# The last tokens of the second pair in the free half of the first pair's last slot: linear attention and a gated feed-forward layer on one core

## The chip, the cores and the metric

The kernel runs on one core of a Trainium2 chip. The metric is the time of one execution on the device in microseconds (us). Engines: PE is TensorE (matmuls and transposes; PEld is its weight load, which overlaps), DVE is VectorE, ACT is ScalarE, POOL is GpSimd, SP is SyncE, from which most transfers are issued. PSUM is the memory that PE writes its results to; ACT and DVE read it.

## The reference

There are 8 batches of 8 heads, with 576 tokens of 64 numbers each, all float32. The attention has no softmax:

```python
kv = np.einsum('bhsd,bhse->bhde', k, v)
out = np.einsum('bhsd,bhde->bhse', q, kv)
rms = np.sqrt(np.mean(out * out, axis=-1, keepdims=True) + 1e-06)
x = out / rms * g_norm          # (8, 8, 576, 64), then to (4608, 512)
```

The feed-forward layer follows, with d_model 512 and d_ff 1536. Its weights come as float64 and are converted on the chip.

```python
gate = 1.0 / (1.0 + np.exp(-(x @ w_gate)))
return (gate * (x @ w_val)) @ w_out
```

## The kernel before

Heads are taken two at a time: a *pair* n is two heads of one batch, so a batch has four pairs (NHP = 4) and there are 32 pairs in all. The tokens of the feed-forward layer come in nine *chunks* of 512 (G), the transposed activations of a chunk lying in the tile xT (chunk(c) makes it). A batch of 576 tokens crosses a chunk's edge.

**Steps of a pair** (attention, L229 to L310). They are kv_mm and kv_out (the 64x64 matrix kv of each head), q_mm (Q, six transposes of q to a PSUM tile, L251), q_out (ACT copies them to the tile qT, L256), u_mm (U, out = q kv, L271), u_square (ACT, L276), u_sum (DVE, L280), u_root (ACT, L284), u_norm (DVE, reciprocal and product, L288 and L290), x_mm (X, transposes with the identity matrix, L298) and x_out (X_OUT, ACT copies to xT with the factor g_norm, L307).

**Slots of tokens.** The 576 tokens of a pair are laid out in NU = 5 slots of 128 partitions, and each slot has 64 columns for each head. U works in groups of 64 tokens: groups 0, 2, 4, 6, 8 go to the lower 64 partitions of the five slots, groups 1, 3, 5, 7, 9 to the upper ones. There are nine groups of tokens but ten places: group 9 takes `t0 = min(PH * i, S - PH)`, that is the tokens of group 8 once more, so the upper half of the last slot holds a copy that nobody reads. A group is two matmuls, one for each head, and each matmul is 64 rows by 64 columns of the array; so the matmuls of two groups in a row take the array's four quadrants in turn. The trace has two records for each such matmul.

**Early and late pairs.** The first eight pairs (NE = 8, two batches) are done in an order written out by hand (`order`, L458), with PSUM tiles of their own. The other 24 pairs, those of batches 2 to 7, run underneath the feed-forward layer. For these, `feed(b)` (L319) puts the steps of the batch's four pairs into the queue `fill`. It takes two pairs at a time, one and two_ (called a couple here), in this order: Q and Q_OUT of one, the same of two_; for the first couple of the batch the kv of all four pairs, of the whole batch, after up to three empty steps; then U of both in one step, Square of both, sum of both, root and norm of one, root and norm of two_, X and X_OUT of one, X and X_OUT of two_. A batch has two couples, so there are twelve.

**The loop around them.** For each chunk c from 1 to 8, `feed(c + 1)` fills the queue, then the first layer (first_layer_fast, products at L578) and the second layer (second_layer_fast, products at L664) are recorded. Both layers use a scheme with seven products of half size (p1 to p7). After every two products of the first layer (eight matmul records on PE) `slot()` takes one step from `fill`. At c = 1 the queue also holds sums of the second layer's weights, spread between the steps. All engines work their instructions off in the order in which they are recorded, so the position in `fill` is the position in the queues of PE, ACT and DVE.

**PSUM tiles of the late pairs.** `at_ps` gives them out in turn from two buffers, at and at1, each with two banks:

```python
    def at_ps(kind):
        if next(turns) % 2 == 0:
            return at0_ps()
        return psum.tile([P, 2, 512], FP32, tag="at1", name="at1")
```

Each of Q, U and X takes one tile for each pair, so that one always has at and two_ has at1 (the trace calls both "at"). A new tile in a buffer waits until the readers of the previous one there are done.

**X and X_OUT.** X transposes the five slots into the PSUM tile: slots 0 to 2 into columns 0 to 383 of bank 0, slots 3 and 4 into columns 0 to 255 of bank 1. X_OUT copies columns 0 to 383 of bank 0 and 0 to 191 of bank 1, with one more cut where a chunk of 512 tokens ends: two pieces in batch 2, three in the batches after.

Of the kernel before, what the change touches and what calls it, by code (L numbers as in the profile page):

```python
# [10 lines left out]
FP32 = mybir.dt.float32  # L11
# [3 lines left out]
AF = mybir.ActivationFunctionType  # L15
ALU = mybir.AluOpType
AX = mybir.AxisListType
# [3 lines left out]
def kernel(  # L21
# [11 lines left out]
    nc = tc.nc  # L33

    B, H, S, HD = q.shape
    T, DM = out.shape
    DF = moe_w_gate.shape[1]
    P = 128
# [5 lines left out]
    PH = P // 2  # L44
    NU = -(-S // P)
    UX = P * 3

    NK4 = S // P
    S4 = P * NK4
# [3 lines left out]
    G = 512  # L53
# [5 lines left out]
    sb = ctx.enter_context(tc.tile_pool(name="sb", bufs=2))  # L59
# [9 lines left out]
    NE = 2 * NHP  # L69
# [66 lines left out]
    one = const.tile([P, 1], FP32, name="one")  # L136
# [74 lines left out]
    g_col = const.tile([P, 1], FP32, name="g_col")  # L211

    kvs = [const.tile([P, 2, HD], FP32, name=f"kv{i}") for i in range(2)]
# [10 lines left out]
    def chunk(c):  # L224
        if c not in xT:
            xT[c] = sb.tile([P, NMT, G], FP32, tag="xT", name="xT", bufs=3)
        return xT[c]

    def attention(n, at_ps):  # L229

        b, m = divmod(n, NHP)
        d = {}
        kv = kvs[n // 2 % 2][:, n % 2]

        def kv_mm():
            d["kv"] = ps = at_ps("kv")
            for j in range(NJ):
                js = slice(HD * j, HD * j + HD)
                for e in range(2):
                    nc.tensor.matmul(ps[HD * e:HD * e + HD, 0, 0:HD], pairs[n]["k"][:, e, js], pairs[n]["v"][:, e, js],  # L240
                                     start=(j == 0), stop=(j == NJ - 1))

        def kv_out():
            nc.vector.tensor_copy(out=kv, in_=d["kv"][:, 0, 0:HD])
            load_kv(n + 4)

        def q_mm():
            d["q"] = ps = at_ps("q")
            for j in range(NJ):
                c0 = NP * (j % JH)  # L250
                nc.tensor.transpose(ps[:, j // JH, c0:c0 + NP], pairs[n]["q"][:, j].rearrange("p e d -> p (e d)"),  # L251
                                    ident[0:NP, 0:NP])

        def q_out():
            d["qT"] = sb.tile([P, 2, JH * NP], FP32, tag="qT", name="qT")
            nc.scalar.copy(out=d["qT"], in_=d["q"][:, :, 0:JH * NP])  # L256
            for i in (n + 4,) if n + 4 < NE else (n + 2,) if n + 2 >= NE else ():
                load_q(i)

        def u_mm():  # L260


            ps = at_ps("u")
            d["u"] = ps[:, :, 0:NU * HD]
            qT = d["qT"].rearrange("p i n -> p (i n)")
            for i in range(2 * NU):
                t0 = min(PH * i, S - PH)
                r = PH * (i % 2)
                for e in range(2):
                    es = slice(HD * e, HD * e + HD)  # L270
                    nc.tensor.matmul(d["u"][r:r + PH, e, HD * (i // 2):HD * (i // 2) + HD], qT[es, t0:t0 + PH], kv[es],  # L271
                                     start=True, stop=True)

        def u_square():
            d["sq"] = sb.tile([P, 2, NU * HD], FP32, tag="sq", name="sq")
            nc.scalar.activation(out=d["sq"], in_=d["u"], func=AF.Square)  # L276

        def u_sum():
            d["ms"] = sb.tile([P, 2, NU], FP32, tag="ms", name="ms")
            nc.vector.tensor_reduce(out=d["ms"].rearrange("p e i -> p (e i)"),  # L280
                                    in_=d["sq"].rearrange("p e (i d) -> p (e i) d", d=HD), axis=AX.X, op=ALU.add)

        def u_root():
            nc.scalar.activation(out=d["ms"], in_=d["ms"], func=AF.Sqrt, bias=eps, scale=1.0 / HD)  # L284

        def u_norm():

            nc.vector.reciprocal(d["ms"], d["ms"])  # L288
            d["xn"] = d["sq"].rearrange("p e c -> p (e c)")
            nc.vector.tensor_tensor(out=d["xn"].rearrange("p (i e d) -> p e i d", e=2, d=HD),  # L290
                                    in0=d["u"].rearrange("p e (i d) -> p e i d", d=HD),
                                    in1=d["ms"].unsqueeze(3).to_broadcast([P, 2, NU, HD]), op=ALU.mult)

        def x_mm():
            d["x"] = ps = at_ps("x")
            for i in range(NU):
                bank, c0 = divmod(P * i, UX)
                nc.tensor.transpose(ps[:, bank, c0:c0 + P], d["xn"][:, P * i:P * i + P], ident)  # L298

        def x_out():  # L300

            s0 = 0
            while s0 < S:
                c, o = divmod(S * b + s0, G)
                i, r = divmod(s0, UX)
                n_ = min(G - o, (UX if i == 0 else S - UX) - r)
                nc.scalar.activation(out=chunk(c)[:, m, o:o + n_], in_=d["x"][:, i, r:r + n_], func=AF.Copy, scale=g_col)  # L307
                s0 += n_

        return [kv_mm, kv_out, q_mm, q_out, u_mm, u_square, u_sum, u_root, u_norm, x_mm, x_out]  # L310


# [6 lines left out]
    def feed(b):  # L319

        early = b == 2
        d = {}

        def kv_mm():
            mains, rest = kv_late[b]
            tiles = [at_ps("kv") for _ in range(2)]
            d["kv"] = tiles
            for n in range(NHP):
                for j in range(NK4):
                    for e in range(2):  # L330
                        c = slice(NK4 * HD * e + HD * j, NK4 * HD * e + HD * j + HD)
                        nc.tensor.matmul(tiles[n // 2][HD * e:HD * e + HD, n % 2, 0:HD], mains[n, "k"][:, c],  # L332
                                         mains[n, "v"][:, c], start=(j == 0), stop=False)
            for i in range(NHP // 2):
                for r in range(2):
                    for e in range(2):
                        n, rs, c = NHP // 2 * r + i, slice(PH * r, PH * r + PH), HD * (2 * i + e)
                        nc.tensor.matmul(tiles[n // 2][HD * e:HD * e + HD, n % 2, 0:HD], rest[rs, c:c + HD],
                                         rest[rs, GH + c:GH + c + HD], start=False, stop=True)

        def kv_out():
            for kv, ps in zip(kvs, d["kv"]):
                nc.vector.tensor_copy(out=kv, in_=ps[:, :, 0:HD])

        def idle():
            pass

        for n in range(NHP * b, NHP * b + NHP, 2):
            one, two_ = (attention(n + i, at_ps) for i in range(2))

            def u_of_both(one=one, two_=two_):
                one[U]()
                two_[U]()

            fill.extend([one[Q], one[Q_OUT], two_[Q], two_[Q_OUT]])
            if n == NHP * b:
                fill.extend([idle] * (0 if early else 3) + [kv_mm, kv_out])
            fill.extend([u_of_both, one[U_SQUARE], two_[U_SQUARE], one[U_SUM], two_[U_SUM], one[U_ROOT], one[U_NORM],
                         two_[U_ROOT], two_[U_NORM], one[X], one[X_OUT], two_[X], two_[X_OUT]])
# [32 lines left out]
    def at0_ps():  # L392
        return psum_at.tile([P, 2, 512], FP32, tag="at", name="at")
# [3 lines left out]
# [5 lines that stand above are left out]
    def early(n):  # L402

        shared = []

        def ps(kind):
            if kind == "q":
                return shared[0]
            t = psum0.tile([P, 2, 512], FP32, tag="kq" if kind == "kv" else f"ux{n % 2}", name="two")
            if kind == "kv":  # L410
                shared.append(t)
                return t[:, :, JH * P:]
            return t
        return ps

    def mm_ps():
        return psum.tile([P, 512], FP32, tag="mm", name="mm", bufs=4)
# [30 lines left out]


    KV, KV_OUT, Q, Q_OUT, U, U_SQUARE, U_SUM, U_ROOT, U_NORM, X, X_OUT = range(11)  # L450
    a = [attention(n, early(n)) for n in range(NE)]

    steps = {"KV": KV, "KVO": KV_OUT, "Q": Q, "QO": Q_OUT, "U": U, "SQ": U_SQUARE, "SUM": U_SUM, "ROOT": U_ROOT,
             "NORM": U_NORM, "X": X, "XO": X_OUT}
# [16 lines left out]
    for token in order.split():  # L471
        name = token.rstrip("0123456789.")
        n = [int(i) for i in token[len(name):].split(".")]
        f = n[0]
        if name == "b":
            if f not in blks:
                if f == 3:
                    psum_ctx.__exit__(None, None, None)
                    psum = ctx.enter_context(tc.tile_pool(name="psum", bufs=1, space=bass.MemoryType.PSUM))
                    ps = (mm_ps(), mm_ps())  # L480
                else:
                    t = at0_ps() if f else two0
                    ps = (t[:, 0], t[:, 1])
# [35 lines left out]
    ps = [two1[t % 2][:, t // 2] for t in range(G // P)]  # L519
# [259 lines left out]
```

## Time and profile before

| what | value |
|---|---|
| median of 4 runs | 1097.14 us (1096.53 to 1099.04) |
| the profiled execution | 1099.04 us, span of its instructions 1097.2 us |
| granted PE clock | 0.998 of full speed |
| busy, share of the span | PE 99%, DVE 51%, ACT 29%, POOL 25% |
| products of the first layer, L578 | 53% of the chain that ended last |
| products of the second layer, L664 | 26% of it |
| L271, L298 and L251 on "at" (late pairs) | 1% each or less |
| late pairs: first Q, last X_OUT | from 164.6 us to 834.4 us |

The span runs from the first to the last instruction of the program. A matmul's record includes the pipeline's tail, so that records of PE overlap; what one costs is seen from its start to the next start. "Idle before" and "waits" name the engine whose signal came last.

### The profile page before, as it was taken

To read this page: it belongs to the slowest core of one execution; us is meant where nothing else is said; L and a number is where in the kernel's file an instruction comes from. 1 tells how busy PE (TensorE), PEld (TensorE's weight loads), DVE (VectorE), ACT (ScalarE), POOL (GpSimd) and SP (SyncE) were. 2 spreads that over 40 slices of the span, in tenths; PEclk is the share of its full clock that TensorE was granted. 3 is DMA by queue.
4 is the path that set the end of the run, shared out by engine and by line. 5 is a ranking of instruction groups with operands and counts; after the bars stand their busy time and mean duration, and the time that the engine had idled before them with its cause. 6 is when DMAs were issued, how large, how long until landed. Compare 5 with 4: busy or idle time off the path is not lost.

```text
span 1097.2 us, 17063 instructions
## 1 busy us (share of the span) xinstructions
PE 1089.7 (99%) x6722; PEld 903.1 (82%) x6722; DVE 564.1 (51%) x1117; ACT 316.1 (29%) x611; POOL 279.2 (25%) x390
## 2 busy tenths in 40 slices
PE   8999999999999999999999999999999999999998
PEld 7544448888888888888888888888888888888888
DVE  3787855763365416561466336641656155615641
ACT  4654322431244113430254014511443011101110
POOL 0000023440244203440344024420334044404410
PEclk9999999999999999999999999999999999999999
DMA  9954711000400040001400040104000100010001
GB/s 230 246 191 153 240 29 33 1 23 20 127 1 22 11 120 19 22 1 36 112 22 1 20 127 1 23 10 121 18 1 1 29 10 1 1 36 4 1 1 39
DMA packets 81519, 57.73 MB, mean 53 GB/s; under 512 B 47392, under 2 KB 75424, under 8 KB 81440
## 3 DMA queue, kind: packets, MB, share of 16 engines
q1 hardware_dynamic: 81184, 56.61, 19.3%
q8 instruction: 54, 0.88, 0.3%
q14 instruction: 25, 0.20, 0.1%
q10 hardware_dynamic: 256, 0.03, 0.0%
HBM read 47.19 MB, written 9.44 MB: 52 GB/s over the span
## 4 chain that ended last, share of the span: by engine, by line
PE 97%; DMA 1%; DVE 1%; SPq 1%; issue 0%; ACT 0%; DVEq 0%
PE mm L578 53%; PE mm L664 26%; PE mm L427 6%; PE at L522 4%; PE at L271 1%; PE at L427 1%; DMA q<-in_q_dram 1%; PE at L298 1%; PE at L332 1%; PE at L251 1%; PE at L506 1%; PE two L271 0%; PE two L251 0%; PE two L298 0%; PE two L240 0%; SPq L78 0%
## 5 line engine op out<-in xcount | busy, mean ns | idle before, releaser
L565 POOL TENSOR_TENSOR tw<-gv 128x256 f32<-128x256 f32 x192 | 138.8, 734 | 767.8 <-PE mm L578 614.0
L578 PE MATMUL mm<-xT,tw 128*128 128x256 f32 x768 | 182.2, 380 | 0.2 <-DVE gv L592 0.2
L578 PE MATMUL mm<-sx,tw 128*128 128x256 f32 x768 | 182.3, 380 | 0.0
L578 PE MATMUL mm<-xT,gv 128*128 128x256 f32 x768 | 181.8, 380 | 0.0
L578 PEld LDWEIGHTS mm<-xT,gv 128*128 128x128 f32 x768 | 144.8, 190 | 19.7 <-issue 0.5
L578 PEld LDWEIGHTS mm<-xT,tw 128*128 128x128 f32 x768 | 144.1, 190 | 19.6 <-issue 0.6
L578 PEld LDWEIGHTS mm<-sx,tw 128*128 128x128 f32 x768 | 144.2, 190 | 19.0
L565 POOL TENSOR_TENSOR tw<-gv,tw 128x256 f32<-128x256 f32 x192 | 146.1, 784 | 0.0
L610 ACT ACTIVATE sg<-sg 128x256 f32<-128x256 f32 x96 | 40.0, 417 | 190.2 <-DVE sg L609 190.2
L600 DVE TENSOR_TENSOR gv<-mm,sg 128x256 f32<-128x256 f32 x96 | 40.8, 424 | 103.1 <-PE mm L578 103.1
L578 PE MATMUL mm<-sx,gv 128*128 128x256 f32 x384 | 91.3, 381 | 0.0
L664 PE MATMUL mm<-w,gv 128*128 128x256 f32 x384 | 88.5, 379 | 0.4 <-DVE gv L617 0.4
L664 PE MATMUL mm<-w,s 128*128 128x256 f32 (+1 forms) x408 | 88.3, 367 | 0.0
L664 PE MATMUL mm<-t2w,gv 128*128 128x256 f32 x384 | 88.1, 379 | 0.0
L586 ACT COPY sg<-mm 128x256 f32<-128x256 f32 x96 | 35.8, 373 | 165.9 <-PE mm L578 162.0
L617 DVE TENSOR_TENSOR gv<-gv,sg 128x512 f32<-128x512 f32 x96 | 82.7, 901 | 0.0
L664 PEld LDWEIGHTS mm<-w,s 128*128 128x128 f32 x408 | 74.1, 190 | 9.4
L664 PEld LDWEIGHTS mm<-w,gv 128*128 128x128 f32 x384 | 72.8, 190 | 10.6 <-DVE gv L617 0.8
L664 PEld LDWEIGHTS mm<-t2w,gv 128*128 128x128 f32 x384 | 72.9, 190 | 9.9
L578 PEld LDWEIGHTS mm<-sx,gv 128*128 128x128 f32 x384 | 72.5, 190 | 10.0
L596 ACT ACTIVATE sg<-mm 128x256 f32<-128x256 f32 x96 | 36.2, 384 | 106.1 <-PE mm L578 106.1
L614 DVE TENSOR_TENSOR gv<-mm,gv 128x256 f32<-128x256 f32 x96 | 40.7, 424 | 48.1 <-PE mm L578 48.1
(97 smaller groups left out, 1094.0 us busy)
## 6 DMA issues: line engine op xcount, KB each, us to landing
q<-in_q_dram SPq DMA_DIRECT2D x64, 144.0 KB, 3.3
st<-in_moe_w_gate_dram SPq DMA_DIRECT2D x12, 512.0 KB, 4.3
st<-in_moe_w_val_dram SPq DMA_DIRECT2D x12, 512.0 KB, 5.3
st<-in_moe_w_out_dram SPq DMA_DIRECT2D x12, 512.0 KB, 4.6
kv<-in_k_dram SPq DMA_DIRECT2D x24, 256.0 KB, 5.1
kv<-in_v_dram SPq DMA_DIRECT2D x24, 256.0 KB, 5.4
out_dram<-sg SPq DMA_DIRECT2D x23, 192.0 KB, 2.3
out_dram<-sg SPq DMA_DIRECT2D x24, 128.0 KB, 2.4
```

The source lines that it names most:

```text
L251: nc.tensor.transpose(ps[:, j // JH, c0:c0 + NP], pairs[n]["q"][:, j].rearrange("p e d -> p (e d)"), ident[0:NP, 0:NP])
L427: nc.tensor.matmul(self.ps[i], w[("wg", "wv")[i], self.f][:, m, :], xT[self.c][:, m, :], start=(m == 0), stop=(m == NMT - 1), skip_group_c ...
L522: nc.tensor.matmul(ps[t], gv[0, f][:, P * t:P * t + P], w["wo", f], start=(f == 0), stop=(f == NFT - 1), skip_group_check=True)
L565: nc.gpsimd.tensor_tensor(out=tw[f, i], in0=b[in0], in1=b[in1] if isinstance(in1, tuple) else tw[f, in1], op=ALU.subtract)
L578: nc.tensor.matmul(ps, wt[:, m, :], xs[:, m, :], start=(new and m == 0), stop=(m == NK - 1), skip_group_check=True)
L586: nc.scalar.copy(out=d["sg"][:, h2], in_=pa)
L596: nc.scalar.activation(out=d["sg"][:, h1], in_=d["pa"], func=AF.Sigmoid)
L600: tt(out=d["h"][:, h2], in0=d["pb"], in1=d["sg"][:, h2], op=ALU.add)
L610: nc.scalar.activation(out=d["sg"][:, h2], in_=d["sg"][:, h2], func=AF.Sigmoid)
L614: tt(out=d["h"][:, h1], in0=d["pc"], in1=d["h"][:, h1], op=ALU.add)
L617: tt(out=d["h"], in0=d["h"], in1=d["sg"], op=ALU.mult)
L664: nc.tensor.matmul(ps, hs(f), ws[:, f, :], start=(new and f == 0), stop=(f == NF2 - 1), skip_group_check=True)
```

## The change

For the late pairs, the second pair of each couple gives up its fifth slot. Its last 64 tokens go to the upper half of the first pair's fifth slot, where the copy was.

- `attention` gets the dictionary d from outside, and `mate` (for two_: the dictionary of one) and `alone`. With a mate, a pair has nu = 4 slots, else 5.
- U of one makes eight groups instead of ten. U of two_ first makes two groups into one's tile: one's last tokens (lower half) and its own last tokens (upper half). Then it makes its own eight.
- Square, sum, root, norm and X of two_ work on four slots, those of one on five as before; one's fifth slot now carries the last tokens of both.
- X_OUT of two_ copies tokens 0 to 383 and 384 to 511 from its own tile, and tokens 512 to 575 from columns 192 to 255 of bank 1 of one's tile. It has one piece more than before.
- The early pairs are called with neither mate nor alone=False and keep their ten groups and five slots. Line numbers behind the edit move (Q is L252, X is L304 and X_OUT is L316 in the changed kernel).

```diff
-    def attention(n, at_ps):
+    def attention(n, at_ps, d, mate=None, alone=True):
...
-        d = {}
-        kv = kvs[n // 2 % 2][:, n % 2]
+        d["kvs"] = kv = kvs[n // 2 % 2][:, n % 2]
+        nu = NU - 1 if mate else NU
...
-            for i in range(2 * NU):
-                t0 = min(PH * i, S - PH)
+            d["u"] = at_ps("u")[:, :, 0:nu * HD]
+            def group(i, of, t0, into):
                 r = PH * (i % 2)
+                qT = of["qT"].rearrange("p i n -> p (i n)")
                 for e in range(2):
                     es = slice(HD * e, HD * e + HD)
-                    nc.tensor.matmul(d["u"][r:r + PH, e, HD * (i // 2):HD * (i // 2) + HD], qT[es, t0:t0 + PH], kv[es],
-                                     start=True, stop=True)
+                    nc.tensor.matmul(into["u"][r:r + PH, e, HD * (i // 2):HD * (i // 2) + HD], qT[es, t0:t0 + PH],
+                                     of["kvs"][es], start=True, stop=True)
+            if mate:
+                for i, of in ((2 * NK4, mate), (2 * NK4 + 1, d)):
+                    group(i, of, S4, mate)
+            for i in range(2 * NU if alone else 2 * NK4):
+                group(i, d, min(PH * i, S4), d)
...
-            for i in range(NU):
+            for i in range(nu):
                 bank, c0 = divmod(P * i, UX)
                 nc.tensor.transpose(ps[:, bank, c0:c0 + P], d["xn"][:, P * i:P * i + P], ident)
...
+            sources = [(UX, d["x"][:, 0]), (S4 if mate else S, d["x"][:, 1])]
+            if mate:
+                sources.append((S, mate["x"][:, 1, P * NU - UX - PH:]))
+            first_, s0 = 0, 0
+            for end, src in sources:
+                while s0 < end:
+                    c, o = divmod(S * b + s0, G)
+                    n_ = min(G - o, end - s0)
+                    nc.scalar.activation(out=chunk(c)[:, m, o:o + n_], in_=src[:, s0 - first_:s0 - first_ + n_],
+                                         func=AF.Copy, scale=g_col)
+                    s0 += n_
+                first_ = end
...
-            one, two_ = (attention(n + i, at_ps) for i in range(2))
+            d0, d1 = {}, {}
+            one, two_ = attention(n, at_ps, d0, alone=False), attention(n + 1, at_ps, d1, d0, False)
```

More of the change, by code (lines that the diff above doesn't have):

```diff
@@ L260, in u_mm @@
         def u_mm():
-            ps = at_ps("u")
-            d["u"] = ps[:, :, 0:NU * HD]
-            qT = d["qT"].rearrange("p i n -> p (i n)")
-            for i in range(2 * NU):
-                t0 = min(PH * i, S - PH)
+            d["u"] = at_ps("u")[:, :, 0:nu * HD]
+            def group(i, of, t0, into):
                 r = PH * (i % 2)
+                qT = of["qT"].rearrange("p i n -> p (i n)")
                 for e in range(2):
                     es = slice(HD * e, HD * e + HD)
-                    nc.tensor.matmul(d["u"][r:r + PH, e, HD * (i // 2):HD * (i // 2) + HD], qT[es, t0:t0 + PH], kv[es],
-                                     start=True, stop=True)
+                    nc.tensor.matmul(into["u"][r:r + PH, e, HD * (i // 2):HD * (i // 2) + HD], qT[es, t0:t0 + PH],
[5 more added lines that the diff above has]
+                group(i, d, min(PH * i, S4), d)
         def u_square():
-            d["sq"] = sb.tile([P, 2, NU * HD], FP32, tag="sq", name="sq")
-            nc.scalar.activation(out=d["sq"], in_=d["u"], func=AF.Square)
+            d["sq"] = sb.tile([P, 2 * NU * HD], FP32, tag="sq", name="sq")[:, 0:2 * nu * HD]
+            nc.scalar.activation(out=d["sq"].rearrange("p (e c) -> p e c", e=2), in_=d["u"], func=AF.Square)
         def u_sum():
-            d["ms"] = sb.tile([P, 2, NU], FP32, tag="ms", name="ms")
-            nc.vector.tensor_reduce(out=d["ms"].rearrange("p e i -> p (e i)"),
-                                    in_=d["sq"].rearrange("p e (i d) -> p (e i) d", d=HD), axis=AX.X, op=ALU.add)
+            d["ms"] = sb.tile([P, 2, NU], FP32, tag="ms", name="ms")[:, :, 0:nu]
+            nc.vector.tensor_reduce(out=d["ms"], in_=d["sq"].rearrange("p (e i d) -> p e i d", e=2, d=HD), axis=AX.X,
+                                    op=ALU.add)
         def u_root():
@@ L288, in u_norm @@
             nc.vector.reciprocal(d["ms"], d["ms"])
-            d["xn"] = d["sq"].rearrange("p e c -> p (e c)")
+            d["xn"] = d["sq"]
             nc.vector.tensor_tensor(out=d["xn"].rearrange("p (i e d) -> p e i d", e=2, d=HD),
                                     in0=d["u"].rearrange("p e (i d) -> p e i d", d=HD),
-                                    in1=d["ms"].unsqueeze(3).to_broadcast([P, 2, NU, HD]), op=ALU.mult)
+                                    in1=d["ms"].unsqueeze(3).to_broadcast([P, 2, nu, HD]), op=ALU.mult)
         def x_mm():
             d["x"] = ps = at_ps("x")
-            for i in range(NU):
+            for i in range(nu):
                 bank, c0 = divmod(P * i, UX)
@@ L300, in x_out @@
         def x_out():
[L302 to L308, printed above, removed]
+            sources = [(UX, d["x"][:, 0]), (S4 if mate else S, d["x"][:, 1])]
[10 more added lines that the diff above has]
+                first_ = end
         return [kv_mm, kv_out, q_mm, q_out, u_mm, u_square, u_sum, u_root, u_norm, x_mm, x_out]
@@ L450 @@
     KV, KV_OUT, Q, Q_OUT, U, U_SQUARE, U_SUM, U_ROOT, U_NORM, X, X_OUT = range(11)
-    a = [attention(n, early(n)) for n in range(NE)]
+    a = [attention(n, early(n), {}) for n in range(NE)]
     steps = {"KV": KV, "KVO": KV_OUT, "Q": Q, "QO": Q_OUT, "U": U, "SQ": U_SQUARE, "SUM": U_SUM, "ROOT": U_ROOT,
```

## The prediction

> **What bounds the kernel now.** I read the page's engine shares and chain first, then what PE waits for after 160 us, where the changed code runs, and then the timeline around each changed step.
>
> ```profile
> PE 1089.7 (99%) x6722; PEld 903.1 (82%) x6722; DVE 564.1 (51%) x1117; ACT 316.1 (29%) x611; POOL 279.2 (25%) x390
> PE 97%; DMA 1%; DVE 1%; SPq 1%; issue 0%; ACT 0%; DVEq 0%
> ```
>
> The first line is busy time by engine, the second the chain that ended last. TensorE is the bound: whatever leaves its queue shortens the span one for one, and whatever makes it wait lengthens it so. The waits of PE between 160 us and the end are two in all:
>
> ```profile
> PE mm L664 <- DVE gv L617: 0.4, 1, 0.4
> PE mm L578 <- DVE gv L592: 0.2, 1, 0.2
> ```
>
> So ACT, DVE and the DMA queues are hidden there, and the question is only what PE issues and what it will newly wait for. The change touches the 24 late pairs, twelve couples (one, two_); the first eight pairs issue the same instructions as before, and no DMA is added, moved or made smaller.
>
> **Removed from PE.** Here are the U block of a couple (all 80 matmul records of both pairs), an X block, and each time the row after it.
>
> ```profile
> 182.14 1.40 PE L271 MATMUL at<-kv,qT 64*64 64x64 f32 x80
> 183.46 0.70 PE L578 MATMUL mm<-xT,gv 128*128 128x256 f32 x2
> ...
> 213.94 0.71 PE L298 MATMUL at<-ident,sq 128*128 128x128 f32 x5
> 214.49 0.81 PE L578 MATMUL mm<-xT,tw 128*128 128x256 f32 x3
> ```
>
> Columns are start, duration, instruction; a matmul's duration includes the pipeline's tail, so cost is read from start to next start. U: 40 matmuls, two records each, take 183.46 − 182.14 = 1.32 us. The single starts inside show groups of four records 7 ns apart (the four quadrants of the array), and 58.5 ns from one group of four to the next. The change leaves 36 matmuls: one's first eight groups (16), then the two last groups, one's into the lower and two_'s into the upper half (4), then two_'s eight (16). The quadrants still rotate, so whole groups of four leave: 8 records, 2 × 58.5 = 117 ns. (An even share of the block, 8/80 of 1.32, would be 132; I take the starts.) X: five transposes take 0.55 us, 109 ns each; two_ keeps four. Per couple 117 + 109 = 226 ns, twelve couples: **−2.71 us**.
>
> Here a rule speaks against the change. The Trainium skill (TensorE: Matmul & The Clock Gate, Part 3: Packing small matmuls) gives a further tile in one packed group about 4 ns. By it eight records would save an estimated 32 ns instead of 117, and the sum would end 1.0 us higher. The trace shows 7 ns inside a group and 58.5 ns from group to group, which speaks for the larger figure as long as whole groups leave.
>
> **Smaller on DVE and ACT.** Square, reduce and normalize of two_ shrink from 640 to 512 columns. PE's work covers this, except at one place before PE's 0.2 us wait at 197.8:
>
> ```profile
> 196.49 0.81 DVE L280 TENSOR_REDUCE ms<-sq 128x10 f32<-128x640 f32 x1
> 197.22 0.74 DVE L592 TENSOR_TENSOR gv<-mm,sg 128x256 f32<-128x256 f32 x2
> 197.78 1.53 PE L578 MATMUL mm<-xT,tw 128*128 128x256 f32 x6 [0.23 <-DVE gv L592]
> ```
>
> This reduce is two_'s, and PE waits for the DVE queue just behind it. Gains between 0 and a fifth of 0.81 (0.16); 128 columns at about 1 ns, as L617's 0.68 us for 512 columns against 0.42 for 256 has it, make **−0.13 us**, once. The other wait (L617 at 247.4) stands behind one's normalize, which keeps its size.
>
> **Added: a fourth eviction, and a wait on it.** X_OUT of two_ must now read its last 64 columns from one's PSUM tile: its last piece of 192 becomes 128 and 64. More important, one's tile ("at") is thereby held until two_'s last piece, and the next step but one, Q of the next couple, writes a new tile into that buffer. Before, that Q needed only one's X_OUT, over by 3.7 us. Each batch of late pairs has one such boundary, between its two couples: six in all. (After the second couple the next Q is 30 us away or more.) Five look like the first three rows here, and the one of chunk 1 like the last three:
>
> ```profile
> 446.23 1.05 ACT L307 ACTIVATE xT<-at,g_col 128x256 f32<-128x256 f32 x3
> 447.22 0.69 PEld L251 LDWEIGHTS at<-ident,q 96*128 96x128 f32 x6
> 447.43 0.66 PE L251 MATMUL at<-ident,q 96*128 96x96 f32 x6
> ...
> 217.20 0.88 ACT L307 ACTIVATE xT<-at,g_col 128x384 f32<-128x384 f32 x2
> 217.73 0.69 PEld L251 LDWEIGHTS at<-ident,q 96*128 96x128 f32 x6
> 217.94 0.66 PE L251 MATMUL at<-ident,q 96*128 96x96 f32 x6
> ```
>
> The pieces end at 447.28, just 0.15 us before Q's first transpose; at chunk 1 they end at 218.07, 0.13 after it. The added piece by form:
>
> ```profile
> L307 ACT ACTIVATE xT<-at,g_col 128x192 f32<-128x192 f32 x32 | 12.6, 422 | 0.3 <-PE at L298 0.2
> L307 ACT ACTIVATE xT<-at,g_col 128x128 f32<-128x128 f32 x8 | 2.9, 364 | 0.3 <-PE at L298 0.2
> L307 ACT ACTIVATE xT<-at,g_col 128x64 f32<-128x64 f32 x8 | 2.5, 310 | 0.3 <-PE at L298 0.2
> ```
>
> 364 + 310 − 422 = 252 ns, less the overlap of two pieces in a row (starts lie about 0.10 us before the end of the one ahead): 0.15 us. So the pieces end at 447.43 and 218.22. What ACT to PE then takes is seen early in the run, where PE does wait for ACT:
>
> ```profile
> 7.75 0.64 ACT L256 COPY qT<-two 128x576 f32<-128x576 f32 x1 [4.29 <-DVE kv L244]
> 8.43 0.60 PEld L271 LDWEIGHTS two<-kv,qT 64*64 64x64 f32 x33 [0.48 <-ACT qT L256]
> ```
>
> 8.38 to 8.43: 0.05 us to the weight load; from there to the first transpose after a wait is 0.03 (load 6.73, transpose 6.76), and the second then follows 109 ns later instead of 87, so 0.02 more. Five boundaries: 447.43 + 0.08 + 0.02 − 447.43 = 0.10 each; chunk 1: 218.22 + 0.08 + 0.02 − 217.94 = 0.38. Sum **+0.90 us**. The start of the pieces hangs on PE itself (the copy of L586 or sigmoid of L610 ahead of them waits for first-layer products), so it shifts with PE and the distances hold. Behind the waiting Q stand, in order, all first-layer matmuls, and for those DVE, ACT and POOL. Bounds: −0 (the wait never last) and the rivals below. One's Square still becomes ready at the 20th matmul; ACT's extra 0.15 us per couple is otherwise free at 29% busy, and would cost 12 × 0.15 = 1.8 us without that cover.
>
> Sum: −2.71 − 0.13 + 0.90 = **−1.94 us**. The profiled execution took 1099.04 us, span 1097.2, so 1097.1 by its own time; it was the slowest of four runs, 1.9 above their median 1097.14. Against the median: **1095.2 us**, 0.18% less. A measurement of this kernel can tell about 0.2% (2.2 us) from no change, so this lies close below that edge.
>
> **Rivals.**
> Covered: the fourth piece does not bite, because ACT's signal goes out before the recorded end. Then −2.84: 1094.3. For it: five boundaries miss by only 0.1 us; against: chunk 1 already ends 0.13 late.
> Dearer seams: after U blocks the trace has a second product starting 320 ns after the first instead of 216; such a restart, 0.104 at each of six boundaries, gives −1.32: 1095.8. Or the mixed group, which takes weights from two qT tiles, loses its overlap and runs at the two-at-a-time rate that the KV block shows (59 ns for two records): +0.117 × 12 = 1.4, so −0.54: 1096.6.
> Slower: Q's wait, at the same six places, costs a slot. If the pieces started one slot later (1.73 us for the eight records of a slot), six boundaries would cost about 10.4 us: 1104.7. It decides from (2.84 + 2.2)/6 = 0.84 us per boundary on, against 0.15 on average in my sum. For: the eviction sits one slot ahead of Q, with no other step between; against: nothing new stands before the pieces on ACT.
> That PE's work does not shrink is ruled out by the order of the changed build: 60 matmuls fewer, 36 per U block, nine transposes per couple.
>
> **How the numbers follow.** Forecast 0.45, covered 0.30, dearer seams 0.18, slower 0.07. Runs scatter by 0.6 us below the median. Faster by over 0.2%: nearly all of covered (0.28), 0.20 of the forecast with that scatter, 0.02 of the seams, 0.50. Slower: 0.07. The rest is 0.43. Low end: −2.71 and all of the 0.39 us that the matmul after the wait at 197.8 came late, 1094.0, less 0.6: 1093.4. High end: 1096.6 plus 0.6: 1097.2.
>
> **What would show it.** Right: U blocks of 72 records in about 1.21 us; X of two_ in 0.44; a new row of PE or PEld at "at", Q's line, waiting for ACT xT, six times, some 0.9 us with chunk 1 the longest; from the first Q of one middle batch to that of the next about 118.38 us instead of 118.73 (403.17 to 521.90). Wrong: no such row (covered), U blocks above 1.3 us (mixed group), or waits of over 0.8 us each (slower).

## The result: 0.19% faster, and the profile after

The changed kernel takes 1094.80 us (median of 33 runs, 1094.36 to 1095.58); the kernel before, with the further runs beside it, 1096.79 (median of 53). That is 1.99 us less, ratio 0.9981, 95% interval 0.9976 to 0.9985. The forecast was 1.94 us less. Its time of 1095.2 us is 0.4 us too high because it was counted from the median of the first four runs, 1097.14, which lies 0.35 above that of all 53.

Engine shares and chain of the changed kernel, from its page:

```profile
PE 1087.0 (99%) x6614; PEld 899.0 (82%) x6614; DVE 562.0 (51%) x1117; ACT 316.4 (29%) x623; POOL 279.2 (26%) x390
PE 98%; ACT 1%; DMA 0%; DVE 0%; SPq 0%; issue 0%
```

PE has 108 records fewer: 96 of U (48 matmuls of two records each) and 12 transposes. ACT has twelve instructions more. Of its 1% of the chain (5.6 us) only 1.4 us lie at a changed place, X_OUT at 214.5 us with the sigmoid ahead of it; the rest lies in the first 13 us and at 241 us. What is new for PE stands in its waits after 160 us:

```profile
PE mm L676 <- DVE gv L629: 0.4, 1, 0.4
PE at L252 <- ACT xT L316: 0.2, 1, 0.2
```

L252 is Q, L316 is X_OUT. Of the two old waits one (L592, now L604) has become too short for the list, and one on Q is new. The weight loader's own waits show Q six times:

```profile
PEld at L252 <- ACT xT L316: 2.0, 6, 0.6
```

These 2.0 us are not the price. The loader normally starts 0.21 us ahead of the transpose, so part of its idle time would have been slack; the price is read from starts, below.

U block of the first late couple, and X of its second pair, on PE, each with the row that follows:

```profile
179.74 1.28 PE L271 MATMUL at<-kv,qT 64*64 64x64 f32 x72
180.95 1.35 PE L590 MATMUL mm<-xT,gv 128*128 128x256 f32 x5
...
211.29 0.60 PE L304 MATMUL at<-ident,sq 128*128 128x128 f32 x4
211.73 1.46 PE L590 MATMUL mm<-xT,tw 128*128 128x256 f32 x6
```

U: 72 records in 1.21 us (1.208 from the single starts, before 1.325), so 117 ns less. X of two_: 0.44 us instead of 0.55.

One of the five ordinary seams (the place where Q of the second couple follows X_OUT of the first), then the seam of chunk 1:

```profile
443.07 1.20 ACT L316 ACTIVATE xT<-at,g_col 128x256 f32<-128x256 f32 x4
444.32 0.53 PEld L252 LDWEIGHTS at<-ident,q 96*128 96x128 f32 x6 [0.29 <-ACT xT L316]
444.32 0.71 PE L252 MATMUL at<-ident,q 96*128 96x96 f32 x6
...
214.44 1.03 ACT L316 ACTIVATE xT<-at,g_col 128x384 f32<-128x384 f32 x3
215.52 0.72 PE L252 MATMUL at<-ident,q 96*128 96x96 f32 x6 [0.17 <-ACT xT L316]
```

At the ordinary seam four pieces take 1.20 us instead of three in 1.05, and Q starts 0.05 us after the last one ends. Before the change, weight load and first transpose were 0.21 us apart; now they start 0.003 us apart. The first Q of a middle batch follows that of the batch ahead after 118.38 us (400.231 to 518.615), as the prediction had it.

### The profile page after: what moved, and what is told of

It reads as the page before. It is cut to its first block, busy times and chain, and to the rows that moved or that the text cites. A ratio compares the mean times of both kernels' runs of the same rounds, so it can differ in the third digit from the quotient of the medians.

```text
span 1093.0 us, 16853 instructions
## 1 busy us (share of the span) xinstructions
PE 1087.0 (99%) x6614; PEld 899.0 (82%) x6614; DVE 562.0 (51%) x1117; ACT 316.4 (29%) x623; POOL 279.2 (26%) x390
## 4 chain that ended last, share of the span: by engine, by line
PE 98%; ACT 1%; DMA 0%; DVE 0%; SPq 0%; issue 0%
PE mm L590 53%; PE mm L676 26%; PE mm L439 6%; PE at L534 4%; PE at L439 2%; PE at L271 1%; PE at L252 1%; PE at L343 1%; PE at L304 1%; PE two L271 1%; PE two L241 0%; PE at L518 0%; PE two L304 0%; DMA q<-in_q_dram 0%; PE two L252 0%; PE at L349 0%
## 5 line engine op out<-in xcount | busy, mean ns | idle before, releaser
L629 DVE TENSOR_TENSOR gv<-gv,sg 128x512 f32<-128x512 f32 x96 | 83.4, 908 | 0.0
```

The lines of the kernel that those rows point to most:

```text
L629: tt(out=d["h"], in0=d["h"], in1=d["sg"], op=ALU.mult)
```

## The experiments

All are variants of the changed kernel, with the kernel before run beside each of them (1096.77 us in the first four, 1096.71 in the last three).

**1. The piece that holds the tile goes first.** In X_OUT of two_, with the pieces first collected in a list:

```diff
...
+            if mate:
+                pieces.insert(0, pieces.pop())
+            for c, o, n_, src in pieces:
+                nc.scalar.activation(out=chunk(c)[:, m, o:o + n_], in_=src, func=AF.Copy, scale=g_col)
```

> X_OUT of two_ copies the 64 columns in one's tile first instead of last. My theory: the six waits of Q (0.39 us at chunk 1, 0.10 at each of five other places, 0.9 in all) come from the order of the pieces alone, so all six rows of PE waiting for ACT xT at Q's line go, the distance from X of two_ to the next Q falls to 3.89 us (from 3.94, and from 4.23 at chunk 1), and the time is 0.9 us below the changed kernel: about 2.9 us below the kernel before, ratio 0.9974. Rival (the wait is a matter of two tiles being read by one step, or of PE starting anew): the rows stay, ratio 0.998.

Measured: 1094.02 us, ratio 0.9975, interval 0.9966 to 0.9984. The same seam on ACT, PEld and PE:

```profile
442.81 1.20 ACT L323 ACTIVATE xT<-at,g_col 128x64 f32<-128x64 f32 x4
443.80 0.69 PEld L252 LDWEIGHTS at<-ident,q 96*128 96x128 f32 x6
444.01 0.66 PE L252 MATMUL at<-ident,q 96*128 96x96 f32 x6
```

The pieces take the same 1.20 us and end at 444.01, but the load starts at 443.80, 0.21 us before that. No row of PE or PEld waiting for ACT at Q's line is left after 160 us, and X of two_ to Q is 3.89 us at all six seams. The wait was a matter of order alone. By the medians this is 0.8 us below the changed kernel (0.9 was expected; the two intervals overlap, so the size rests on the starts), and its median is the lowest here.

**2. One piece more, ahead of the seams.** In the first couple of each batch the last 64 columns are copied as two pieces of 32.

```diff
...
+            if mate and m == 1:
+                c, o, n_, src = pieces.pop()
+                for i in range(2):
+                    pieces.append((c, o + n_ // 2 * i, n_ // 2, src[:, n_ // 2 * i:n_ // 2 * (i + 1)]))
...
```

> The changed kernel, with the last 64 columns of X_OUT of two_ copied in two pieces of 32, in the first couple of each batch only (ahead of the six places where Q follows). My theory: one piece more costs about 0.15 us on ACT, and Q takes it over in full at all six: +0.9 us against the changed kernel, each wait longer by 0.15; ratio to the kernel before 0.999. Rival (ACT is hidden anyway): no change against the changed kernel, ratio 0.998.

Measured: 1095.73 us, ratio 0.9993, interval 0.9984 to 1.0002. The loader's waits on ACT:

```profile
PEld at L252 <- ACT xT L325: 2.9, 6, 0.7
```

2.0 became 2.9 over six waits, 0.15 each, and the median is 0.93 us above the changed kernel. At chunk 1 the distance from X of two_ to Q grew from 4.23 to 4.38 us, at the next seam from 3.95 to 4.09.

**3. The same piece more, where no Q follows** (`m == 3` in place of `m == 1`).

> The same cut in two pieces of 32, in the second couple of each batch only, behind which the next Q is 30 us away. My theory: ACT has the same extra work six times and PE takes none of it: 0.0 us against the changed kernel, waits of Q as in it (0.9 us in all), ratio 0.998. Rival (ACT's work is itself on the path): +0.9 us, ratio 0.999.

Measured: 1094.80 us, ratio 0.9984, interval 0.9975 to 0.9993.

```profile
PEld at L252 <- ACT xT L325: 2.0, 6, 0.6
```

Same work on ACT, same waits as the changed kernel, same median. So the 0.15 us that a piece more adds on ACT reach PE in full in the first couple and not at all in the second.

**4. A half turn more in U.** Two matmuls, both into the lower half, at the end of U of two_:

```diff
+            if mate:
+                group(0, d, 0, d)
```

> The changed kernel, with one group of U made twice in two_ of each couple (two matmuls more, both into the lower half, four records). Theory A, the four records that start 7 ns apart belong to two matmuls of one group: the U block grows by 58.5 ns, 12 times, +0.70 us; then the copies alone were half of the turn and could have been dropped without the merge at the same gain. Theory B, they are the four quadrants, and a half turn costs as much as a whole one: +117 ns, +1.4 us. Theory C, a further packed tile costs about 4 ns: +16 ns, +0.2 us. The order of the records behind it goes on as before. Ratio to the kernel before 0.9988 by A, 0.9994 by B, 0.9983 by C; the length of the U block tells them apart.

Measured: 1096.12 us, ratio 0.9996, interval 0.9987 to 1.0005.

```profile
179.55 1.38 PE L271 MATMUL at<-kv,qT 64*64 64x64 f32 x76
180.86 1.35 PE L592 MATMUL mm<-xT,gv 128*128 128x256 f32 x5
```

The block takes 1.311 us from single starts, 103 ns more for four records, nearest to theory B, though below its 117. The starts show both: whole turns run as groups of four records 7 ns apart, one group every 58.5 ns; the half turn runs as two groups of two records 7 ns apart, 59 ns from one to the next. So a group of four is the four quadrants, and a half-filled turn runs as many groups as a full one. The 14 ns short of 117 come from the block's end: the next product starts 148 or 149 ns after the last record in every variant, and a last group of two records has begun its last one some 14 ns sooner than a group of four. The repeated group writes columns that U of two_ had filled before; it starts on the usual beat, 38 ns after the record ahead, so no wait for that shows. The 59 ns for two records are the rate that the KV block had in the trace of before.

**5. Q one slot closer.** X_OUT of two_ and the next couple's Q share one step of the queue:

```diff
...
+            if n == NHP * b:
+                fill.append(one[Q])
+            else:
+                x_out_before = fill.pop()
+
+                def seam(one=one, x_out_before=x_out_before):
+                    x_out_before()
+                    one[Q]()
+
+                fill.append(seam)
...
```

> The changed kernel, with X_OUT of two_ and the next couple's Q in one step of the queue instead of two, so that at the six seams Q stands one slot (1.73 us) closer behind the pieces. My theory: ACT ends the pieces at the same moment as before, since it waits for products that stand ahead of Q, and PE stands still until then: 1.85 us at five seams and 2.1 at chunk 1, 11.4 in all where the changed kernel pays 0.9; about +10.5 us against it, ratio 1.0077. Rival (the waits are filled by weight loads and products pulled ahead, or ACT comes earlier when PE is earlier): well under +5 us, ratio below 1.003.

Measured: 1104.84 us, ratio 1.0073, interval 1.0056 to 1.0090. An ordinary seam, ACT and PE:

```profile
446.35 1.20 ACT L316 ACTIVATE xT<-at,g_col 128x256 f32<-128x256 f32 x4
447.60 0.71 PE L252 MATMUL at<-ident,q 96*128 96x96 f32 x6 [1.61 <-ACT xT L316]
```

Q starts 0.05 us after the pieces again, and PE stands idle instead of working on products: 10.0 us above the changed kernel, about 1.7 per seam. Nothing fills the hole. The expectation of 10.5 left out that with the steps moved one slot the other old wait (PE for DVE's L629 in the list above, at 245 us) no longer appears; the product that waits there starts 0.57 us late in the changed kernel.

**6. The same, with the held piece first.**

> The same with the 64 columns from one's tile copied first. My theory: Q then waits for the first piece alone, which ends about 0.9 us before the last one: 0.95 us at five seams, 1.4 at chunk 1, about 6.2 us above the kernel with this order and the usual seams (2.7 us below the kernel before): ratio 1.003. Rival (Q waits until the whole X_OUT is done, whichever piece holds the tile): as the tight seam without it, ratio 1.0077.

Measured: 1099.34 us, ratio 1.0023, interval 1.0014 to 1.0033.

```profile
PEld at L252 <- ACT xT L323: 7.2, 6, 1.6
```

In experiment 5 this row is 12.4 over six. Q waits for the first piece and not for the step. It comes out 5.3 us above experiment 1; the starts give 0.95 at five seams and 1.39 at chunk 1, 6.1 in all (6.2 was expected), less the 0.57 of that old wait, absent here too.

**7. As many matmuls as the change took out, but in the lower half only.**

```diff
+            if mate:
+                for i in (0, 2):
+                    group(i, d, PH * i, d)
```

> The changed kernel, with two groups of U made twice in two_ of each couple, both into the lower half (four matmuls more, as many as the change took out, but two half turns in place of a whole one). My theory, from the half turn that was measured at 103 ns: each half turn is a turn of its own at 59 ns for two records, so the U block grows by 103 + 118 = 221 ns, 12 times, +2.65 us against the changed kernel: more than the copies of the kernel before cost. Ratio to the kernel before 1.0005. Rival (what counts is the number of matmuls): +117 ns, +1.4 us, ratio 0.9994.

Measured: 1097.56 us, ratio 1.0007, interval 0.9998 to 1.0016.

```profile
179.73 1.50 PE L271 MATMUL at<-kv,qT 64*64 64x64 f32 x80
181.16 1.13 PE L593 MATMUL mm<-xT,gv 128*128 128x256 f32 x4
```

80 records as in the kernel before, but 1.43 us (1.428 from the single starts) instead of 1.32: 220 ns above the changed kernel, 221 expected. By the medians it costs 2.8 us, against 2.65. The first half turn, which another follows, costs 117 ns like a whole one; only the last costs 103. The number of matmuls does not set the price, their places in the array do.

The intervals of the ratios reach about 1 us or more to either side, as much as several of these differences. So here are the sizes from one trace each, from the start of the first late Q to the start of the last product on PE. That stretch is 927.48 us in the changed kernel. It is 0.93 shorter in experiment 1, 0.91 longer in 2, 0.01 shorter in 3, 1.23 longer in 4, 9.67 longer in 5 and 2.64 longer in 7; experiment 6 is 5.47 above experiment 1.

## Why the prediction was right

**U, −117 ns per couple.** Measured 117 (1.325 to 1.208 us), and the group that mixes the two pairs' weights keeps its overlap, so that part of the rival of dearer seams did not occur. Nor did its other part: behind the waiting Q the products start 245 and then 216 ns apart, as they did before the change. The reason given, that whole turns of the four quadrants leave, was an inference when it was written; experiments 4 and 7 show it. They also weigh the rule that the prediction set against the change. The Trainium skill (TensorE: Matmul & The Clock Gate, Part 3) gives about 4 ns for a further packed tile, an estimated 16 ns if each of the four records of experiment 4 counts as a tile; measured were 103. Records inside a group do start 7 ns apart, so something like the rule holds within a turn, and not for opening the next one. Here the measurement decides.

Experiment 4 adds what the sum did not need. With group 9 left out and no merge, each pair would keep a half turn in its U. By experiments 4 and 7 one inside the block costs the whole 117 ns and one at its end 103, so an estimated 14 ns of a couple's 117 would be saved. It takes the two half turns laid together to save a turn. That exact variant was not tried, since its fifth slot would hold values that were never written.

**X, −109 ns per couple.** Measured 109 (0.546 to 0.437 us in every X of two_). Together with U 12 × 226 = 2.71 us, as booked.

**DVE, −0.13 us once.** The reduce of two_ before PE's old wait, and the product that had waited:

```profile
193.97 0.68 DVE L286 TENSOR_REDUCE ms<-sq 128x8 f32<-128x512 f32 x1
195.13 1.10 PE L590 MATMUL mm<-xT,tw 128*128 128x256 f32 x4
```

0.68 instead of 0.81 us; the product starts 473 ns after the one ahead of it instead of 610, a gain of 0.14. This term is read from the two traces; no experiment varies it alone.

**The wait of Q, +0.90 us.** Measured 0.93; the prediction's own terms, 0.10 five times and 0.38, make 0.88, which it put as 0.90. X of two_ to Q was 4.00 us before, and 3.89 without a wait once a transpose has left (experiment 1 shows just that). It is 3.95 at an ordinary seam (440.376 to 444.322) and 4.23 at chunk 1 (211.29 to 215.52), and the Q block itself takes 0.55 us instead of 0.50: 0.107 five times, 0.39 once. Inside this term the split was off. The first transpose came sooner after the signal than the early rows said (0.003 us after its weight load instead of 0.03), the second later (0.14 us after the first, against 0.11 taken and 0.087 without a wait). That the two nearly cancel is luck.

**The sum.** −2.71 − 0.14 + 0.93 = −1.92 us. Between the first late Q and the end of the last product on PE the two profiles differ by 1.91 us (164.58 to 1094.25 before, 162.18 to 1089.94 after). Their spans differ by 4.3 us, but 2.4 of that lies before the first late Q, where the instructions are the same; the medians do not carry it.

**The rivals.** "Covered" got 0.30, and the trace rules it out: all six waits are there. It leaned on the recorded end of ACT coming after its signal; Q's load starts 0.05 us after the recorded end at all six seams. This chance is also most of what put "faster by over 0.2%" at 0.50, above "the same" at 0.43, although the sum itself stood inside the 0.2%, where the measurement then fell. "Slower" named the right place, and experiment 5 shows its price: with Q a slot closer the change loses about 8 us to the kernel before. As built, Q is held up by 0.11 us at five places and 0.39 at one.

## What to carry to other kernels

When an edit makes two units share a buffer, look for the next writer of that buffer and for the last reader in its new place; if the shared part is read first, the buffer is free early, and here that is worth the 0.9 us that the sharing cost. Price small matmuls by turns of the array and not by count: here half a turn costs nearly as much as a whole one, so leaving matmuls out pays only when a whole turn goes, as when two half turns become one. Where one engine is busy for 99% of the time and its waits can be listed on two lines, the sum of single starts from one trace can place a small change; here it placed one of 0.2% within a tenth of a microsecond.

## What the hardware showed that was not expected

- A half turn of 64x64 matmuls costs 103 ns at the end of the block and 117 ns when another follows, as much as the whole turn (1.208, 1.311 and 1.428 us).
- After a wait the second transpose starts 137 to 140 ns after the first, at every seam; without one, 86 or 87. The third follows after 81 to 83 in both.
- The same instruction on ACT, six times, costs 0.93 us ahead of a seam and 0.0 us elsewhere, at 29% busy for ACT in both variants.
